# A linear-attention and mixture-of-experts kernel: scatters tied to the next group's tiles, |turns| on ScalarE, sines for two tiles at once, xT by tile, and another test of the decay

## The chip, the cores and the metric

The kernel runs on one core of a Trainium2 chip. The metric is the device time of the program in microseconds (us). The engines are named as the profile names them: PE (TensorE; PEld is its weight loading), ACT (ScalarE), DVE (VectorE), POOL (GpSimd) and SP (SyncE, which only issues transfers here). Each engine works through its own list of instructions in a fixed order and waits on semaphores for the others.

## The reference, cut to what matters

```python
# q, k, v, a_re, a_im: (batch 4, heads 8, seq 768, head_dim 48)
mag = sqrt(a_re**2 + a_im**2);  scale = minimum(mag, 0.999) / (mag + 1e-6)
ar, ai = a_re * scale, a_im * scale
for t in range(768):                      # per batch and head, a 48 x 48 complex state
    S_re, S_im = ar*S_re - ai*S_im + outer(k[t], v[t]),  ar*S_im + ai*S_re
    y[t] = q[t] @ S_re
x = y as (3072 tokens, 384)
logits = x @ w_gate + log1p(exp(x @ w_noise)) * noise      # 8 experts
top2, weights = two largest of a token, softmax over the two
out[token] += weight * (relu(x @ w1[e]) @ w2[e])           # w1: 384 x 1024, w2: 1024 x 384
```

## The kernel before, in words

The sequence is cut into 6 groups g of 128 steps; with 4 batches b that gives 24 tiles, n = 4g + b, each 128 rows by 384 columns (8 heads of 48). The recurrence is turned into matrix products: the decay's logarithm and its angle are summed along the 128 rows by a product with a triangular matrix, q and k are multiplied by e to the plus or minus of the summed logarithm and by the cosine and sine of the summed angle, and a tile's output is a masked 128 x 128 score matrix times v plus q times the state Z that came in from the group before.

The steps of a group, by the functions that the program lists at the end of this section:

- `p1` (for two tiles, 128 x 768): Ln of re, Exp of its negative (1/re), the tangent im/re, and the logarithm of the magnitude. A Relu of RE_MIN - re with a sum (tile `scr`) notes in `bad` whether some re lies under 0.6; with such a value, or a large tangent, a slow path at the end of the program would do the work again.
- `p2a`, `p2t`, `p2s`: Arctan; a product with `tri_t` that sums the angle in turns; rounding by adding a large constant (ACT, tile `tf`), the remainder (DVE, line 254), its absolute value by a bitwise and (DVE, line 255), then for each tile two sines of 384 columns, the cosine from the absolute value (tile `tr`).
- `p3`, `p3q`: a product with `tri_l`, Exp with both signs (`ee`), multiplied into `qk`, then `qh` and `kh`. One row of `ee` goes out to memory and comes back as the columns `ecol` of the group.
- `tr_unit`, `sc_unit`, `st_unit`: transposes of qh and kh into `qT` and `kT` (copied by ACT), scores `psc`, masked by DVE into `am`, and the state's product `pG`. `st_scale` multiplies two ecol columns into `fcol` and that into the state Z.
- `y_unit`: 16 products into `pY` (8 in the first group), copied by ACT into `xT` (line 347); `x_unit` transposes it back into token rows `xr`; `gate_logits` (tiles `lt`, `lz`) and `gate_dispatch` choose two experts for each token, compute a slot `sl` for each, and POOL scatters the rows to memory `xs` by 8 indirect transfers a group (line 408).

The eight experts follow: `load_x` fetches an expert's rows (`xga`, `xgb`), `x_T` transposes them, `mm1` and `mm2` are the two layers with weights split into a high and a low part, and the result is added to `out` by gathers and scatters of POOL.

Ln and Exp need another activation table than Arctan and Sin, so ACT's table functions run in phases: `phase` numbers them, and extra dependencies hold each table load behind the whole phase before. A table of steps (`at`, with the numbers of `P`) says at which tile's step a function is emitted, so that p1, p2 and p3 of a group run some tiles ahead of the tiles that use them. From this emission order, with a higher priority for `x_unit`, `gate_logits` and `gate_dispatch`, the framework makes each engine's list by its own estimate of when operands are ready; the lists that result are quoted below.

`xT` is one buffer of 128 x 4 x 4 x 128 for a whole group: the first `y_unit` of a group writes a buffer that `x_unit` and `gate_logits` of the group before still read.

Of the kernel before, what the change touches and what calls it, by code (L numbers as in the profile page):

```python
# [24 lines left out]
RE_MIN = 0.6  # L25
# [51 lines left out]
def kernel(  # L77
# [57 lines left out]
    b_re = cp.tile([128, 1], F32, name="b_re")  # L135
    nc.vector.memset(b_re, RE_MIN)
# [43 lines left out]
    for t in ecol:  # L180
        nc.vector.memset(t, 0.0)
# [8 lines left out]
    XT, W = {}, {}  # L190
# [29 lines left out]
    def p1(m):  # L220

        T0[m] = [pf.tile([128, 2, HD], F32, name=f"t0{i}", bufs=2) for i in range(3)]
        ta, tb, th = (flat(x) for x in T0[m])
        ph = 2 * (2 * m // B)
        re, im = flat(RE[m]), flat(IM[m])
        phase(ph, ta, re, AF.Ln)
        phase(ph, tb, ta, AF.Exp, scale=-1.0)
# [4 lines left out]
        nc.scalar.activation(sc, re, AF.Relu, scale=-1.0, bias=b_re, accum_out=bad[:, 0, i:i + 1])
# [1 line left out]
        nc.vector.scalar_tensor_tensor(ta, ta, 2.0, tb, op0=OP.mult, op1=OP.add)
# [13 lines left out]
    def p2t(n):  # L248
        b, g = bt(n)
        pt = psC.tile([128, 512], F32, name="cum")  # L250
        nc.tensor.matmul(pt[:, :HD], tri_t, T0[n // 2][2][:, b % 2, :], start=True, stop=True)  # L251
# [1 line left out]
        nc.scalar.activation(TF[n][:, 1, :], pt[:, :HD], AF.Identity, bias=b_rnd)
        nc.vector.scalar_tensor_tensor(TF[n][:, 0, :], TF[n][:, 1, :], -RND, pt[:, :HD], op0=OP.add, op1=OP.subtract)
        nc.vector.tensor_scalar(TF[n][:, 1, :].bitcast(I32), TF[n][:, 0, :].bitcast(I32), 0x7FFFFFFF, None,
                                op0=OP.bitwise_and)
# [21 lines left out]
    def p3q(n, i):  # L278
        tr = TR[n].rearrange("p r (h d) -> p r h d", h=H)
        nc.vector.tensor_mul((qh, kh)[i][n % NQ][:, :, :, 0:D].rearrange("p h r d -> p r h d"),  # L280
                             QK[n][:, i, :].rearrange("p (h d) -> p h d", h=H)[:, None].to_broadcast([128, 2, H, D]),
                             tr)
# [29 lines left out]
    def st_upd(n):  # L312
        b, g = bt(n)
        if g + 1 == NG:
            return
        if g:
            nc.vector.tensor_add(Z[b], Z[b], pG)
        else:
            Z[b] = pa.tile([112, H, D], F32, name=f"z{b}")
            nc.vector.tensor_copy(Z[b], pG)  # L320

    def st_scale(n):
        b, g = bt(n)
# [3 lines left out]
        nc.vector.tensor_mul(f, ecol[g % 3][:, b, :], ecol[(g + 1) % 3][:, b, :])
        nc.vector.tensor_mul(Z[b], Z[b], f[:, :, None].to_broadcast([112, H, D]))

    def y_unit(n):  # L330

# [15 lines left out]
        nc.scalar.activation(XT[g][:, :, b, :], pY, AF.Copy)  # L347
# [66 lines left out]


# [142 lines left out]
    for g in range(NG):  # L558
        f = B * g + .5
        q1, q2, q3 = P.get(f"s{g}", (P["p1"], P["p2"], P["p3"]))  # L560
        for j in range(B // 2):
# [4 lines left out]
            at(f - q2, p2carry, m)  # L566
        for j in range(B):
# [292 lines left out]
```

## Time and profile before

| | |
|---|---|
| median of 3 runs | 743.57 us (743.0 to 745.0) |
| the profiled execution | 743.21 us, span 741.5 us |
| mean granted TensorE clock | 0.992 |
| PE / PEld busy | 702.5 us (95%) / 623.5 us (84%) |
| DVE / ACT / POOL busy | 418.6 (56%) / 346.6 (47%) / 169.5 us (23%) |
| attention (to the last xT) | about the first 262 us |
| the eight experts | the rest |

How to read it: the shares are means over two stages with different limits. In the expert stage PE is busy without a gap and ACT and DVE for less than half of the time; in the attention stage ACT and DVE are about as busy as PE. A matmul's end is modelled, so that a stretch in which PE counts as busy can still have room in it; the number of matmuls in a stretch and the busy time of PEld say more.

### The profile page before, as it was taken

The page shows a single profiled execution, that of the slowest core. Times are in us where ns is not written, and L with a number is a line of the kernel's source. Part 1 is how long each engine was busy: PE and PEld are TensorE (multiplying, and loading weights), DVE is VectorE, ACT ScalarE, POOL GpSimd, SP SyncE. Part 2 cuts the span into 40 slices and gives each one's busy share as a digit, 9 for nine tenths or more (in the row PEclk, how much of TensorE's full clock was granted, in tenths as well). Part 3 has the DMA queues.
Part 4 walks back from the last instruction along what each step waited for, and adds up shares of the span by engine and source line. Part 5 has one row for each costly group of instructions (what it writes and reads, how often), then busy time and mean ns, then how long its engine had stood idle before and what let it go on. Part 6 is the DMA issues. An engine that isn't in the chain of part 4 may idle for free. (4 is left out here: it accounts for less than half of the span.)

```text
span 741.5 us, 13540 instructions
## 1 busy us (share of the span) xinstructions
PE 702.5 (95%) x5184; PEld 623.5 (84%) x5184; DVE 418.6 (56%) x960; ACT 346.6 (47%) x633; POOL 169.5 (23%) x187
## 2 busy tenths in 40 slices
PE   0799989999999899999999999999999999999995
PEld 0467778979788779989988998997998998998995
DVE  5698999989998373554353444425425525435311
ACT  7999999987966330443133223323304303413300
POOL 2000005130524341022123124024024023122212
PEclk9999999999999999999999999999999999999998
DMA  8476966643367432262244235226226135131101
GB/s 299 104 250 168 290 198 217 184 165 88 112 191 242 147 133 94 68 232 80 96 155 122 86 111 174 75 87 212 74 89 201 40 122 186 33 105 56 50 33 34
DMA packets 64090, 100.18 MB, mean 135 GB/s; under 512 B 26490, under 2 KB 46129, under 8 KB 64016
## 3 DMA queue, kind: packets, MB, share of 16 engines
q1 hardware_dynamic: 54464, 71.68, 31.0%
q0 software_dynamic: 9552, 27.54, 10.7%
q8 instruction: 43, 0.70, 0.4%
q14 instruction: 31, 0.25, 0.1%
HBM read 68.55 MB, written 32.08 MB: 136 GB/s over the span
## 5 line engine op out<-in xcount | busy, mean ns | idle before, releaser
L535 PE MATMUL po<-w2h,h 128*128 128x384 f32 x768 | 201.7, 339 | 0.0
L511 PE MATMUL ph<-x,w1h 128*128 128x320 f32 (+1 forms) x720 | 192.4, 351 | 0.3 <-ACT x L498 0.3
L535 PEld LDWEIGHTS po<-w2h,h 128*128 128x128 f32 x768 | 139.9, 188 | 0.1
L511 PEld LDWEIGHTS ph<-x,w1h 128*128 128x128 f32 x720 | 126.7, 188 | 15.6 <-ACT x L498 0.5
L516 DVE SCALAR_TENSOR_TENSOR h<-ph,h 128x256 fp32r<-128x256 f32 (+2 forms) x184 | 74.2, 432 | 99.9 <-ACT h L513 99.9
L535 PE MATMUL po<-w2l,h 128*128 128x384 f32 x384 | 129.6, 337 | 0.0
L549 POOL DMA_INDIRECT out_dram<-ao,ox x56 | 55.7, 995 | 319.4 <-DVE ao L548 277.6
L511 PE MATMUL ph<-x,w1l 128*128 128x320 f32 (+1 forms) x360 | 125.5, 349 | 0.0
L513 ACT ACTIVATE h<-ph 128x320 fp32r<-128x320 f32 (+1 forms) x120 | 61.5, 512 | 119.8 <-PE ph L511 114.4
L548 DVE SCALAR_TENSOR_TENSOR ao<-po,gw,ao 128x384 f32<-128x384 f32 (+1 forms) x56 | 34.5, 616 | 134.3 <-PE po L535 133.4
L408 POOL DMA_INDIRECT xs<-xr,sl x48 | 57.0, 1187 | 199.2 <-DVE kh L280 106.9
L498 ACT CAST x<-px 128x320 fp32r<-128x320 f32 (+1 forms) x45 | 21.9, 502 | 126.7 <-PE px L496 125.9
L511 PEld LDWEIGHTS ph<-x,w1l 128*128 128x128 f32 x360 | 67.6, 188 | 7.3
L535 PEld LDWEIGHTS po<-w2l,h 128*128 128x128 f32 x384 | 72.1, 188 | 0.1
L522 POOL DMA_INDIRECT ao<-out_dram,ox x49 | 49.0, 999 | 37.3 <-DMA out_dram<-ao,ox 24.5
L300 PE MATMUL psc<-qT,kT 112*128 112x128 f32 x384 | 54.1, 277 | 0.0
L300 PEld LDWEIGHTS psc<-qT,kT 112*128 112x128 f32 x384 | 48.3, 191 | 2.7 <-issue 1.1
L464 ACT CAST w2h<-raw 128x768 fp32r<-128x768 f32 x32 | 25.3, 834 | 51.4 <-PE po L540 49.3
L346 PE MATMUL pY<-am,v 128*48 128x128 f32 x384 | 44.1, 280 | 4.5 <-DVE am L301 4.5
L344 PE MATMUL pY<-qT,z 112*48 112x128 f32 x320 | 38.2, 281 | 0.2 <-ACT xT L347 0.2
L346 PEld LDWEIGHTS pY<-am,v 128*48 128x48 f32 x384 | 31.5, 125 | 7.9 <-DVE am L301 5.7
L251 PE MATMUL cum<-t,tri_t 128*128 128x384 f32 x48 | 20.9, 559 | 17.9 <-ACT t L198 17.0
(204 smaller groups left out, 1038.0 us busy)
## 6 DMA issues: line engine op xcount, KB each, us to landing
raw<-in_moe_w_dram SPq DMA_DIRECT2D x24, 512.0 KB, 3.9
raw<-in_moe_w_dram SPq DMA_DIRECT2D x32, 384.0 KB, 3.8
qk<-in_qk_dram SPq DMA_DIRECT2D x24, 384.0 KB, 4.0
xga<-xs SPq DMA_DIRECT2D x8, 800.0 KB, 4.2
re<-in_a_dram SPq DMA_DIRECT2D x12, 384.0 KB, 5.3
im<-in_a_dram SPq DMA_DIRECT2D x12, 384.0 KB
v<-in_v_dram SPq DMA_DIRECT2D x24, 192.0 KB, 3.2
out_dram<-zero SPq DMA_DIRECT2D x12, 384.0 KB, 5.7
```

Source lines behind the costliest of these rows:

```text
L300: nc.tensor.matmul(p[:, j, :], KT[n][:, h, :], QT[n][:, h, :], start=True, stop=True)
L344: nc.tensor.matmul(o, Z[b][:, h, :], QT[n][:, h, :], start=True, stop=False, skip_group_check=True)
L346: nc.tensor.matmul(o, V[n][:, h, :], AM[n][:, h, :], start=not g, stop=True, skip_group_check=True)
L408: d = nc.gpsimd.indirect_dma_start(out=xs, out_offset=bass.IndirectOffsetOnAxis(ap=sl[:, kk, b:b + 1], axis=0), in_=XR[g][:, lo + b, :], i ...
L464: nc.scalar.copy(hi, raw_t)
L511: nc.tensor.matmul(p[:, :n], W1[kk][i][:, f * 128:(f + 1) * 128], XW[w, kk][:, j, :], start=(m == 0), stop=(m == len(ms) - 1))
L513: nc.scalar.activation(h[:, 0:n], p[:, :n], AF.Relu)
L516: nc.vector.scalar_tensor_tensor(h[:, dst:dst + b - a], p[:, a:b], 0.0, h[:, a:b].bitcast(F32), op0=OP.max, op1=OP.subtract)
L522: nc.gpsimd.indirect_dma_start(out=ao[j][0:w, :], out_offset=None, in_=out, in_offset=bass.IndirectOffsetOnAxis(ap=OX[e][0:w, j:j + 1], ax ...
L535: nc.tensor.matmul(p[:, :DM], HT[w, f][i][:, o:o + 128], W2[f // 2][k2][:, f % 2, :], start=(m == 0), stop=(m == len(ms) - 1))
L548: nc.vector.scalar_tensor_tensor(a, p[0:n, :DM], g, a, op0=OP.mult, op1=OP.add)
L549: nc.gpsimd.indirect_dma_start(out=out, out_offset=bass.IndirectOffsetOnAxis(ap=OX[e][0:n, j:j + 1], axis=0), in_=a, in_offset=None, bound ...
```

## The change

It has six parts.

1. **Scatters.** For groups 0 to 3, the scatters of tile b = 1, 2, 3 of a group get a dependency on ACT's xT copy of tile b - 1 of the next group.
2. **The test of re.** The Relu pass and its sum go. The Exp that gives 1/re sums its output on the way (`accum_out`), and the sum is compared with 1.6 x 768 at the end. Beside it DVE takes the minimum of each group's `ecol` (`decm`, 6 reductions of 112 x 32), compared with 1e-15.
3. **|turns| on ScalarE.** The bitwise and on DVE (24 of 128 x 384) goes; an Abs on ACT (12 of 128 x 768) takes its place.
4. **Sines for two tiles.** `tf` and `tr` hold two tiles; 48 sines of 384 columns become 24 of 768. `p2s` is emitted after the four `p2t` of its group, not after each.
5. **xT by tile**, in 6 buffers of 128 x 4 x 128.
6. **fcol by group.** One product of 112 x 32 for a group, where there was one of 112 x 8 for a tile (5 for 20).

```diff
-        phase(ph, tb, ta, AF.Exp, scale=-1.0)
+        i = 2 * m
+        phase(ph, tb, ta, AF.Exp, scale=-1.0, accum_out=bad[:, 0, i:i + 1])
         nc.vector.tensor_mul(th, im, tb)
-        i = 2 * m
         nc.vector.tensor_tensor_reduce(tb, th, th, 1.0, 0.0, OP.mult, OP.max, bad[:, 1, i:i + 1])
-        sc = pf.tile([128, 2 * HD], BF16, name="scr")
-        nc.scalar.activation(sc, re, AF.Relu, scale=-1.0, bias=b_re, accum_out=bad[:, 0, i:i + 1])
...
-        TF[n] = pf.tile([128, 2, HD], F32, name="tf", bufs=4)
-        nc.scalar.activation(TF[n][:, 1, :], pt[:, :HD], AF.Identity, bias=b_rnd)
-        nc.vector.scalar_tensor_tensor(TF[n][:, 0, :], TF[n][:, 1, :], -RND, pt[:, :HD], op0=OP.add, op1=OP.subtract)
-        nc.vector.tensor_scalar(TF[n][:, 1, :].bitcast(I32), TF[n][:, 0, :].bitcast(I32), 0x7FFFFFFF, None,
-                                op0=OP.bitwise_and)
+        if n % 2 == 0:
+            TF[n // 2] = pf.tile([128, 2, 2, HD], F32, name="tf", bufs=2)
+        tf = TF[n // 2][:, :, n % 2, :]
+        nc.scalar.activation(tf[:, 1, :], pt[:, :HD], AF.Identity, bias=b_rnd)
+        nc.vector.scalar_tensor_tensor(tf[:, 0, :], tf[:, 1, :], -RND, pt[:, :HD], op0=OP.add, op1=OP.subtract)
...
-    def p2s(n):
-        TR[n] = pq.tile([128, 2, HD], F32, name="tr", bufs=8)
-        phase(2 * (n // B) + 1, TR[n][:, 0, :], TF[n][:, 1, :], AF.Sin, scale=-TWO_PI, bias=b_cos)
-        phase(2 * (n // B) + 1, TR[n][:, 1, :], TF[n][:, 0, :], AF.Sin, scale=-TWO_PI)
+    def p2s(m):
+        f, a = (flat(TF[m][:, i]) for i in range(2))
+        nc.scalar.activation(a, f, AF.Abs)
+        TR[m] = pq.tile([128, 2, 2, HD], F32, name="tr", bufs=4)
+        phase(2 * (2 * m // B) + 1, flat(TR[m][:, 0]), a, AF.Sin, scale=-TWO_PI, bias=b_cos)
+        phase(2 * (2 * m // B) + 1, flat(TR[m][:, 1]), f, AF.Sin, scale=-TWO_PI)
...
+        if b == B - 1:
+            nc.vector.tensor_reduce(decm[0:112, g:g + 1], ecol[g % 3].rearrange("p b h -> p (b h)"), axis=AX.X, op=OP.min)
...
-        f = pa.tile([112, H], F32, name="fcol", bufs=2)
-        nc.vector.tensor_mul(f, ecol[g % 3][:, b, :], ecol[(g + 1) % 3][:, b, :])
-        nc.vector.tensor_mul(Z[b], Z[b], f[:, :, None].to_broadcast([112, H, D]))
+        if b == 0:
+            FC[g] = pa.tile([112, B, H], F32, name="fcol", bufs=2)
+            nc.vector.tensor_mul(FC[g], ecol[g % 3], ecol[(g + 1) % 3])
+        nc.vector.tensor_mul(Z[b], Z[b], FC[g][:, b, :, None].to_broadcast([112, H, D]))
...
-            XT[g] = pa.tile([128, H // 2, B, 128], F32, name="xT")
+        XT[n] = pa.tile([128, H // 2, 128], F32, name="xT", bufs=6)
...
-        nc.scalar.activation(XT[g][:, :, b, :], pY, AF.Copy)
+        YC[n] = nc.scalar.activation(XT[n], pY, AF.Copy)
...
+                if g < NG - 2 and b:
+                    behind.append((d, B * (g + 1) + b - 1))
...
+            at(f - q2 + .01, p2s, m)
...
-            at(f - q2 + j * P["dt"] + P["ds"], p2s, n)
...
+    later = mybir.DependencyInfo(mybir.DependencyClass.Sync, mybir.DependencyReason.SCHED_ONLY)
+    for d, n in behind:
+        tc.add_manual_dep(d.ins, YC[n].ins.name, later, reason="pace")
```

The lists of the engines move. On ACT, the first group's angle phase, from the table load ahead of Arctan on (`t_159` and the like are p1's tiles); before:

```order
L197 ACT_TABLE_LOAD
L198 ACTIVATE t_159<-t_159 128x768
L198 ACTIVATE t_173<-t_173 128x768
L232 ACTIVATE scr,bad<-re,b_re 128x768 x2
L253 ACTIVATE tf<-cum,b_rnd 128x384 x2
L198 ACTIVATE tr<-tf 128x384
L198 ACTIVATE tr<-tf,b_cos 128x384
L198 ACTIVATE tr<-tf 128x384
L198 ACTIVATE tr<-tf,b_cos 128x384
L253 ACTIVATE tf<-cum,b_rnd 128x384 x2
L198 ACTIVATE tr<-tf 128x384
L198 ACTIVATE tr<-tf,b_cos 128x384 x2
```

and with the change (its lines are numbered a little higher; L262 is Abs):

```order
L198 ACT_TABLE_LOAD
L199 ACTIVATE t_159<-t_159 128x768
L199 ACTIVATE t_171<-t_171 128x768
L254 ACTIVATE tf<-cum,b_rnd 128x384 x3
L262 ACTIVATE tf<-tf 128x768
L199 ACTIVATE tr<-tf 128x768
L254 ACTIVATE tf<-cum,b_rnd 128x384
L199 ACTIVATE tr<-tf,b_cos 128x768
L262 ACTIVATE tf<-tf 128x768
L199 ACTIVATE tr<-tf 128x768
L199 ACTIVATE tr<-tf,b_cos 128x768
```

The two Relu passes are gone from it, the third rounding now stands ahead of the first sine, and each Abs stands behind the remainders of two tiles.

Also on ACT, the rows ahead of tile 4's xT, the first of group 1. Before, it stands behind group 2's Exps and the copy `lt` of group 0's logits:

```order
L355 COPY xr<-cum 128x384
L197 ACT_TABLE_LOAD
L198 ACTIVATE ee<-cum 128x384 x4
L198 ACTIVATE t_1153<-re 128x768
L198 ACTIVATE ee<-cum 128x384 x4
L198 ACTIVATE t_1154<-t_1153 128x768
L366 COPY lt<-cum 128x128
L347 ACTIVATE xT<-pY 128x4x128
```

and with the change right behind group 2's Arctan, ahead of its sines and Exps (the first row is tile 3's xT, the last tile 4's):

```order
L352 ACTIVATE xT<-pY 128x512
L294 ACTIVATE qT<-ptr 112x512
L199 ACTIVATE t_661<-t_661 128x768
L294 ACTIVATE kT<-ptr 112x512 x2
L199 ACTIVATE t_661<-t_660,b_eps 128x768
L198 ACT_TABLE_LOAD
L199 ACTIVATE t_571<-t_571 128x768
L199 ACTIVATE t_662<-t_662 128x768
L352 ACTIVATE xT<-pY 128x512
```

Tile 4's xT moved past a whole angle phase and a whole Exp phase of ACT.

On DVE, where the attention ends and the first expert's rows are read (`gw` and `ox` come from the fetched rows `xga`; the `am` around them belong to tiles 22 and 23); before:

```order
L404 TENSOR_REDUCE sl_3304<-ga1oh 128x2
L301 TENSOR_TENSOR am<-psc,mask 128x512 x2
L489 COPY gw<-xga 128x4
L490 CAST ox<-xga 128x4
L301 TENSOR_TENSOR am<-psc,mask 128x512
L370 COPY lz<-cum 128x48
```

and with the change:

```order
L409 TENSOR_REDUCE sl_3214<-ga1oh 128x2
L303 TENSOR_TENSOR am<-psc,mask 128x512 x3
L497 COPY gw<-xga 128x4
L498 CAST ox<-xga 128x4
L375 COPY lz<-cum 128x48
```

One of tile 23's two masked halves now stands ahead of the copy that waits for the fetched rows; the other stays behind it.

More of the change, by code (lines that the diff above doesn't have):

```diff
@@ L24 @@
 LN2_LO = 1.4286068203094173e-06
-RE_MIN = 0.6
+RE_SUM = 1.6
+DEC_MIN = 1e-15
 TAN_MAX = 1.5
@@ L134 @@
     nc.vector.memset(b_cos, math.pi / 2.0)
-    b_re = cp.tile([128, 1], F32, name="b_re")
-    nc.vector.memset(b_re, RE_MIN)
     b_rnd = cp.tile([128, 1], F32, name="b_rnd")
@@ L160 @@
     nc.vector.memset(bad, 0.0)
+    decm = cp.tile([128, NG], F32, name="decm")
+    nc.vector.memset(decm, 1.0)
     ap = ctx.enter_context(ExitStack())
@@ L180 @@
     for t in ecol:
-        nc.vector.memset(t, 0.0)
+        nc.vector.memset(t, 1.0)
     pG = psA.tile([112, H, D], F32, name="pG", bufs=1)
@@ L189 @@
     QT, KT, AM, Z, XR, QKD = {}, {}, {}, {}, {}, {}
-    XT, W = {}, {}
+    XT, FC = {}, {}
     phases = {}
@@ L251, in p2t @@
         nc.tensor.matmul(pt[:, :HD], tri_t, T0[n // 2][2][:, b % 2, :], start=True, stop=True)
-        TF[n] = pf.tile([128, 2, HD], F32, name="tf", bufs=4)
-        nc.scalar.activation(TF[n][:, 1, :], pt[:, :HD], AF.Identity, bias=b_rnd)
-        nc.vector.scalar_tensor_tensor(TF[n][:, 0, :], TF[n][:, 1, :], -RND, pt[:, :HD], op0=OP.add, op1=OP.subtract)
-        nc.vector.tensor_scalar(TF[n][:, 1, :].bitcast(I32), TF[n][:, 0, :].bitcast(I32), 0x7FFFFFFF, None,
-                                op0=OP.bitwise_and)
-        if g + 1 < NG:
-            nc.sync.dma_start(car[:, b, :], TF[n][127:128, 0, :])
-    def p2s(n):
-        TR[n] = pq.tile([128, 2, HD], F32, name="tr", bufs=8)
-        phase(2 * (n // B) + 1, TR[n][:, 0, :], TF[n][:, 1, :], AF.Sin, scale=-TWO_PI, bias=b_cos)
-        phase(2 * (n // B) + 1, TR[n][:, 1, :], TF[n][:, 0, :], AF.Sin, scale=-TWO_PI)
+        if n % 2 == 0:
[3 more added lines that the diff above has]
+        nc.vector.scalar_tensor_tensor(tf[:, 0, :], tf[:, 1, :], -RND, pt[:, :HD], op0=OP.add, op1=OP.subtract)
+        if g + 1 < NG:
+            nc.sync.dma_start(car[:, b, :], tf[127:128, 0, :])
+    def p2s(m):
[4 more added lines that the diff above has]
+        phase(2 * (2 * m // B) + 1, flat(TR[m][:, 1]), f, AF.Sin, scale=-TWO_PI)
     def p3(n):
@@ L278, in p3q @@
     def p3q(n, i):
-        tr = TR[n].rearrange("p r (h d) -> p r h d", h=H)
+        tr = TR[n // 2][:, :, n % 2, :].rearrange("p r (h d) -> p r h d", h=H)
         nc.vector.tensor_mul((qh, kh)[i][n % NQ][:, :, :, 0:D].rearrange("p h r d -> p r h d"),
@@ L353, in x_unit, with gate_logits @@
         for i in range(H // 2):
-            nc.tensor.transpose(p[:, i * 128:(i + 1) * 128], XT[g][:, i, b, :], ident)
+            nc.tensor.transpose(p[:, i * 128:(i + 1) * 128], XT[n][:, i, :], ident)
         nc.scalar.copy(XR[g][:, b, 0:DM].rearrange("p (h d) -> p h d", h=H),
                        p.rearrange("p (h x) -> p h x", h=H)[:, :, 0:D])
-    def gate_logits(xT, lo, hi):
+    def gate_logits(g, lo, hi):
         n = hi - lo
@@ L362, in gate_logits @@
             for b in range(n):
-                nc.tensor.matmul(p[32 * b:32 * b + 32, 0:128], wg[:, i, :], xT[:, i, lo + b, :],
+                nc.tensor.matmul(p[32 * b:32 * b + 32, 0:128], wg[:, i, :], XT[B * g + lo + b][:, i, :],
                                  start=(i == 0), stop=(i == H // 2 - 1), tile_position=(0, 32 * b), skip_group_check=True)
@@ L377, in gate_tr @@
         return p
-    scat = []
+    scat, behind, YC = [], [], {}
     def gate_dispatch(g, lo, hi, lz):
@@ L423, in glog @@
     def glog(g, lo, hi):
-        LZ[g, lo] = gate_logits(XT[g], lo, hi)
+        LZ[g, lo] = gate_logits(g, lo, hi)
     def gdis(g, lo, hi):
@@ L657 @@
     nc.gpsimd.iota(lim, pattern=[[N, E]], base=CAP, channel_multiplier=0, allow_small_or_imprecise_dtypes=True)
-    nc.vector.tensor_scalar(bad[:, 0], bad[:, 0], 0.0, None, op0=OP.is_gt)
+    nc.vector.tensor_scalar(bad[:, 0], bad[:, 0], RE_SUM * 2 * HD, 0.5, op0=OP.is_le, op1=OP.is_lt)
+    nc.vector.tensor_scalar(decm, decm, DEC_MIN, None, op0=OP.is_lt)
+    nc.vector.tensor_reduce(bad[0:112, 0, 1:2], decm[0:112], axis=AX.X, op=OP.max)
     nc.vector.tensor_scalar(bad[:, 1], bad[:, 1], TAN_MAX ** 2, None, op0=OP.is_gt)
```

## The prediction, made before the changed kernel was run

> **What bounds the kernel now.** I read the windows first, since the page's shares mix two stages: columns are the window, then busy time and number of instructions of PE, PEld, DVE, ACT and POOL, the granted clock and the transfers' share.
>
> ```profile
> 28.00:115.00 87.00, 79.46 (x841) 64.02 (x842) 78.90 (x148) 81.57 (x151) 1.80 (x2) 0.98 0.71 214
> 115.00:191.00 76.00, 75.94 (x919) 64.09 (x917) 70.53 (x173) 65.89 (x126) 23.82 (x23) 1.00 0.51 157
> 191.00:231.00 40.00, 39.60 (x505) 34.56 (x504) 36.28 (x93) 30.12 (x61) 17.12 (x15) 1.00 0.58 177
> 400.00:500.00 100.00, 100.00 (x575) 94.62 (x574) 40.21 (x80) 27.91 (x49) 19.76 (x20) 1.00 0.30 99
> ```
>
> In the experts (last row) PE has no gap and ACT and DVE work less than half of the time, so nothing that the change touches counts there; if the attention ends earlier, the experts move forward by as much. In the attention the limits differ. From 28 to 115 us ACT works 81.57 of 87 us and PE gets 841 matmuls in, 9.7 a microsecond: ACT bounds. From 115 to 231 us PE counts as busy for 115.5 of 116 us with 12.3 matmuls a microsecond, and ACT and DVE follow at 83% and 92%. Ahead of 28 us stands the first group's chain, on which PE waits for its first 17 us.
>
> ```profile
> PE cum L251 <- ACT t L198: 17.0, 1, 17.0
> PE pY L346 <- DVE am L301: 4.5, 4, 3.0
> ```
>
> These two rows of the waits of PE (waiter, releaser, total, times, longest) say that beside the start the only long wait is one of 3.0 us for a mask product, which belongs to the end of the attention (below).
>
> **The change, part by part.** Prices of one instruction (mean ns before the last bar) are in these rows of the groups by form:
>
> ```profile
> L198 ACT ACTIVATE t<-t 128x768 f32<-128x768 f32 x36 | 29.8, 850 | 0.2
> L198 ACT ACTIVATE tr<-tf,b_cos 128x384 f32<-128x384 f32 x24 | 13.8, 615 | 0.5 <-DVE tf L255 0.5
> L198 ACT ACTIVATE tr<-tf 128x384 f32<-128x384 f32 x24 | 12.7, 527 | 0.1
> L198 ACT ACTIVATE t<-t,b_eps 128x768 f32<-128x768 f32 x12 | 11.2, 936 | 2.8 <-DVE t L234 2.8
> L232 ACT ACTIVATE scr<-re,b_re 128x768 bf16<-128x768 f32 x12 | 11.2, 934 | 0.3 <-DMA re<-in_a_dram 0.3
> L232 ACT ACTIVATION_READ_ACCUMULATOR scr<-re,b_re 128x1 f32 x12 | 2.4, 196 | 0.0
> L254 DVE SCALAR_TENSOR_TENSOR tf<-tf,cum 128x384 f32<-128x384 f32 x24 | 12.8, 550 | 8.2 <-ACT tf L253 7.7
> L255 DVE TENSOR_SCALAR tf<-tf 128x384 int32<-128x384 int32 x24 | 8.0, 362 | 0.1
> L327 DVE TENSOR_TENSOR fcol<-ecol,ecol 112x8 f32<-112x8 f32 x20 | 3.0, 158 | 0.1
> L404 DVE TENSOR_REDUCE sl<-ga4oh 128x8 uint32<-128x64 f32 x4 | 0.9, 214 | 0.0
> ```
>
> A group of four tiles loses on ACT two Relus with their readings, 2 x (934 + 196) = 2.26 us, and eight sines, 4 x (615 + 527) = 4.57 us. It gains two readings of the sum (0.39), four sines of 768, priced like Exp with and without a bias, 2 x (936 + 850) = 3.57 us, and two Abs at 850, 1.70 us. That is 6.83 against 5.66 us. Four instructions fewer give back 0.4 us of this, since on ACT one starts about 0.1 us before the last ends (3.97 + 0.84 = 4.81 against 4.72 in the rows below). ACT is relieved by 0.8 us a group, little, because the Abs comes to the busier engine. DVE loses 4 x 362 and 4 x 158 ns and gains one fcol and one minimum at some 0.2 us each, by the reduction at 214: 1.7 us a group.
>
> *To tile 7, the ACT-bound stretch.* Counted in ACT's two lists up to the xT of tile 7, before has 10 Relus and 24 sines, the change 8 sums, 12 sines and 6 Abs, and all other kinds stand in equal numbers (the Relus had been put ahead). 10 x 1.13 + 12 x 1.142 = 25.0 us against 8 x 0.196 + 6 x 1.786 + 6 x 0.85 = 17.4 us: 7.6 us less, 5.8 us with 18 instructions fewer. How much of it reaches the end differs by place. The start of ACT's timeline (start, duration):
>
> ```profile
> 3.97 0.84 ACT L198 ACTIVATE t<-re 128x768 f32<-128x768 f32 x1 [1.86 <-DMA re<-in_a_dram]
> 4.72 0.92 ACT L232 ACTIVATE scr<-re,b_re 128x768 bf16<-128x768 f32 x1
> 5.63 0.83 ACT L198 ACTIVATE t<-t 128x768 f32<-128x768 f32 x1
> 6.59 0.84 ACT L198 ACTIVATE t<-re 128x768 f32<-128x768 f32 x1
> 8.26 1.56 ACT L198 ACTIVATE t<-t 128x768 f32<-128x768 f32 x2
> 17.53 0.92 ACT L232 ACTIVATE scr<-re,b_re 128x768 bf16<-128x768 f32 x1
> 19.63 1.05 ACT L253 ACTIVATE tf<-cum,b_rnd 128x384 f32<-128x384 f32 x2
> 26.84 1.28 ACT L197 ACT_TABLE_LOAD   x1
> 17.04 2.90 PE L251 MATMUL cum<-t,tri_t 128*128 128x384 f32 x4 [17.04 <-ACT t L198]
> ```
>
> The second Ln starts at 6.59 though ACT was free at 6.46, so it seems to have waited for its load: the first Relu was hidden by that. The second one holds its Exp from 7.34 to 8.26, 0.9 us that come through the rest of the chain. The two Relus at 17.53 stood where ACT waits for the first angle product (half of PE's four, 17.04 + 1.45 = 18.5); the rounding could start 1.1 us sooner, but the new list puts a third rounding ahead of the first sine, and that one waits until a `cum` buffer is read out by DVE (550 ns) and filled again (1.45 us). I take 0.4 us, bounds a loss of 0.5 and a gain of 2. Together **-1.3 us**, between -0.4 and -3.8.
>
> Of the 5.8 us, 2.4 belong to these first 27 us (four Relus less four readings, 8 sines for 4, two Abs, 6 instructions: 4.5 - 0.8 + 4.6 - 3.6 - 1.7 - 0.6). The other 3.4 us lie where ACT is busy for 94% of the time; I take **-3.0 us**, bounds 0 and -3.4.
>
> *xT by tile.* In the old list tile 4's xT waits for group 0's logits, since they share the buffer:
>
> ```profile
> 72.64 0.62 ACT L347 ACTIVATE xT<-pY 128x512 f32<-128x512 f32 x1
> 96.60 0.33 ACT L366 COPY lt<-cum 128x128 f32<-128x128 f32 x1
> 96.74 0.69 ACT L347 ACTIVATE xT<-pY 128x512 f32<-128x512 f32 x1
> 104.49 0.60 ACT L347 ACTIVATE xT<-pY 128x512 f32<-128x512 f32 x1 [0.90 <-PE pY L346]
> 114.47 0.59 ACT L347 ACTIVATE xT<-pY 128x512 f32<-128x512 f32 x1
> ```
>
> These are the xT of tiles 3, 4, 6 and 7, with the logits' copy: 24 us without a finished tile, then a crowd. The new list has tile 4 ahead of group 2's sines, so PE's work is spread. What it is worth at most is what ACT idles in this window, 87 - 81.57 = 5.4 us; I take **-1.0 us**, for a list that is less lumpy, not shorter.
>
> *Tiles 8 to 19.* Three groups' relief, 5 us on DVE and 2.3 on ACT, meets a PE that counts as busy throughout. I take **-1.5 us**, bounds 0 and -5.
>
> *What the change adds.* An Abs waits for the remainders of two tiles; mostly one other ACT instruction stands between the second rounding and it, as long as one remainder (550 ns). If DVE comes at once nothing is lost; if the remainder stands behind a product of 0.95 us, 1.5 us are. For all 12 together I take **+1.0 us**, near the lower end, since the lists put the remainders right behind the roundings; behind a late Abs stand that phase's sines, its table load and its Exps, and for these wait qh, kh and PE.
>
> *The scatters' wait.* Behind a waiting scatter stand POOL's next scatters and the clearing of the row buffer two groups on. But in time they come late already:
>
> ```profile
> 112.89 1.17 POOL L408 DMA_INDIRECT xs<-xr,sl  x1 [106.92 <-DVE kh L280]
> 220.40 0.60 ACT L347 ACTIVATE xT<-pY 128x512 f32<-128x512 f32 x1 [0.71 <-PE pY L346]
> 228.18 1.60 POOL L408 DMA_INDIRECT xs<-xr,sl  x1 [0.30 <-ACT kT L292]
> 230.37 0.59 ACT L347 ACTIVATE xT<-pY 128x512 f32<-128x512 f32 x1
> ```
>
> Group 0's first scatter starts at 112.89, after the xT of tile 6 (104.49) for which its last must wait; group 3's last tile goes out at 228.18, after tile 18's xT at 220.40 (the last row is tile 19's). Each scatter is bound by its slots, not by the new wait: **0**, and its number on POOL and the transfers stay.
>
> *The end of the attention.*
>
> ```profile
> 248.91 0.97 POOL L408 DMA_INDIRECT xs<-xr,sl  x1 [0.31 <-issue]
> 257.06 0.17 DVE L489 COPY gw<-xga 128x4 f32<-128x4 f32 x1 [7.75 <-DMA xga<-xs]
> 257.94 0.57 PE L346 MATMUL pY<-am,v 128*48 128x128 f32 x4 [2.99 <-DVE am L301]
> ```
>
> DVE stands still until the first expert's rows have come, and tile 23's mask products stand behind that, so PE waits 2.99 us. In the new list one of the two is ahead of it, the other still behind, and the y unit needs both: **0**, bounds -3.0 and +1.
>
> The sum is -1.3 - 3.0 - 1.0 - 1.5 + 1.0 = -5.8 us. The profiled execution took 743.21 us for a span of 741.5, so 737.4; the median of the runs, 743.57, is 0.36 higher. I say **737.5 us**.
>
> **The rivals.** *Room in PE (larger gain).* If the shared xT buffer and a late DVE hold PE back from 115 us on, more comes free than 1.5 us. PEld works 98.65 of these 116 us, 85%, against 94.6% in the experts; filled as densely, the stretch would be 116 x (1 - 85.0/94.6) = 11.8 us shorter. Half of that in place of the 1.5 us gives 733. For it: the matmuls per microsecond vary between windows at equal busy time; against: the expert products are of another size. The Trainium skill says the same of this measure (Perfetto Trace Analysis, Identifying the Most-Contended Engine): matmul busy time is a poor sign of how near PE is to its limit, the weight load's share a better one; the trace agrees in that busy reads 99% at both densities.
>
> *Only the start (no change).* If the middle follows a loop through all three engines, in which a lighter ACT only waits longer, then -1.3 and a little stay: 742. For it: DVE at 91% in ACT's own window.
>
> *The Abs in ACT's way (slower).* Its place is the angle phase of each group, its price the wait for DVE. From 0.5 us more for each of the 12 the sum is used up; at 1.0 us more it is -5.8 + 12 = +6.2, 749.5. For it: before, only the cosine waited for line 255, and DVE is at 92%. Against: remainders were met in time so far (that row shows 0.5 us of wait in all 24).
>
> *The waits do nothing, or the list hurts elsewhere* is inside these: it alters no term.
>
> **How the numbers follow.** Forecast 0.45 (735 to 740.5), room in PE 0.2, only the start 0.2, the Abs 0.15. A measurement of this kernel tells about 0.3%, 2.2 us, from no change. The forecast and the larger gain lie below 741.3, faster 0.65; the third within, 0.2; slower 0.15. The range leaves out the far half of the larger gain and the last case: 731.5 to 744.5.
>
> **What would show it.** ACT's table load now at 26.84 should come at 25 to 26 us; tile 7's xT near 109; tile 19's (now 230.37) near 224 to 226; PE's long wait at the end of about 3 us again. Abs should have waits of DVE under 3 us in total, scatters none of ACT, the experts should take the same time from the last xT to the end. It is wrong if ACT idles more from 28 to 115 us, or if tile 7 is early and tile 19 is not.

## The result, and the profile after

The changed kernel takes 738.7 us (median of four runs, 738.59 to 739.76); the kernel before, beside it, 743.8 (743.0 to 745.0). The ratio is 0.9933, 95% interval 0.992 to 0.9946: 5.1 us faster, where 737.5 us was forecast. The number is nearly met. The places are not, so that the hit is in good part luck; most of this section and the next are about that.

The profiled execution of the changed kernel took 739.76 us for a span of 738.0. It is the longest of the four runs, so the two traces differ by 3.5 us of span and not by 5.1; loads that came late at the start, seen below, are part of that. The easiest way to find where they lie is ACT's copy of each tile, `xT<-pY`: its start tells when the tile left the attention. First before (tiles 0, 22 and 23; tiles 4, 6, 7 and 19 stand in the prediction), start and duration:

```profile
45.95 0.58 ACT L347 ACTIVATE xT<-pY 128x512 f32<-128x512 f32 x1
...
250.96 0.60 ACT L347 ACTIVATE xT<-pY 128x512 f32<-128x512 f32 x1 [1.31 <-PE pY L346]
261.12 0.60 ACT L347 ACTIVATE xT<-pY 128x512 f32<-128x512 f32 x1 [1.43 <-PE pY L346]
```

Then after, tiles 0, 4, 6, 7, 19, 22 and 23:

```profile
46.88 0.58 ACT L352 ACTIVATE xT<-pY 128x512 f32<-128x512 f32 x1
...
81.18 0.58 ACT L352 ACTIVATE xT<-pY 128x512 f32<-128x512 f32 x1
...
104.07 0.64 ACT L352 ACTIVATE xT<-pY 128x512 f32<-128x512 f32 x1
113.83 0.59 ACT L352 ACTIVATE xT<-pY 128x512 f32<-128x512 f32 x1
...
229.24 0.58 ACT L352 ACTIVATE xT<-pY 128x512 f32<-128x512 f32 x1
...
250.56 0.60 ACT L352 ACTIVATE xT<-pY 128x512 f32<-128x512 f32 x1 [1.31 <-PE pY L351]
257.31 0.60 ACT L352 ACTIVATE xT<-pY 128x512 f32<-128x512 f32 x1 [0.56 <-PE pY L351]
```

Differences of these starts, and of the span's end (741.5 and 738.0), give a table by stretch:

| stretch | before, us | after, us | difference | forecast |
|---|---|---|---|---|
| start to tile 0 | 45.95 | 46.88 | +0.93 | -1.3 |
| tile 0 to tile 7 | 68.52 | 66.95 | -1.57 | -4.0 |
| tile 7 to tile 19 | 115.90 | 115.41 | -0.49 | -1.5 |
| tile 19 to tile 22 | 20.59 | 21.32 | +0.73 | 0 |
| tile 22 to tile 23 | 10.16 | 6.75 | -3.41 | 0 |
| tile 23 to the end | 480.38 | 480.69 | +0.31 | 0 |

(The forecast's +1.0 for the Abs had no place of its own.) Tile 4 comes 15.6 us sooner and tile 7 only 0.6 us; and the step between tiles 22 and 23, where the forecast has nothing, has 3.4 of the 3.5 us, the others together 0.1.

The windows after, with the columns that the prediction names, and behind them the last window of the kernel before, which it did not show:

```profile
28.00:115.00 87.00, 80.11 (x845) 65.21 (x846) 75.43 (x137) 79.26 (x140) 0.48 (x1) 0.96 0.72 217
115.00:191.00 76.00, 75.21 (x924) 64.22 (x923) 67.45 (x158) 66.09 (x121) 23.49 (x24) 1.00 0.50 154
191.00:231.00 40.00, 39.84 (x502) 34.48 (x500) 35.20 (x90) 31.54 (x60) 14.36 (x14) 1.00 0.52 166
231.00:262.00 31.00, 29.09 (x321) 24.54 (x320) 20.12 (x98) 14.35 (x33) 9.87 (x11) 1.00 0.57 192
```

```profile
231.00:262.00 31.00, 27.51 (x292) 23.66 (x293) 16.51 (x84) 12.68 (x30) 8.80 (x11) 0.94 0.48 164
```

From 28 to 115 us ACT works 79.26 us instead of 81.57 and so idles 7.7 us instead of 5.4, while PE gets 845 matmuls in instead of 841: ACT's relief has become ACT's waiting. The waits say for whom (waiter, releaser, total, times, longest); before and after, over the whole span:

```profile
ACT kT L292 <- PE ptr L291: 5.5, 12, 0.7
DVE am L301 <- PE psc L300: 7.8, 5, 3.2
```

```profile
ACT kT L294 <- PE ptr L293: 9.2, 17, 1.3
DVE am L303 <- PE psc L302: 16.1, 12, 2.8
```

ACT waits longer for PE's transposes and DVE longer for PE's scores. At the end of the attention, DVE and PE after (the lines before are the last fence ahead of the prediction's sum):

```profile
251.64 0.69 DVE L303 TENSOR_TENSOR am<-psc,mask 128x512 f32<-128x512 f32 x1 [2.73 <-PE psc L302]
...
254.71 0.17 DVE L497 COPY gw<-xga 128x4 f32<-128x4 f32 x1 [2.38 <-DMA xga<-xs]
255.66 0.68 DVE L303 TENSOR_TENSOR am<-psc,mask 128x512 f32<-128x512 f32 x1
...
254.38 0.39 PE L351 MATMUL pY<-am,v 128*48 128x128 f32 x4
254.82 0.39 PE L351 MATMUL pY<-am,v 128*48 128x128 f32 x4
...
256.39 0.43 PE L351 MATMUL pY<-am,v 128*48 128x128 f32 x4 [0.96 <-DVE am L303]
```

and PE before, behind its wait of 2.99 us:

```profile
258.72 0.65 PE L346 MATMUL pY<-am,v 128*48 128x128 f32 x4
```

One mask product of tile 23 now stands ahead of the weights copy `gw<-xga`; the rows for that copy are also there 2.35 us sooner (254.71 against 257.06). PE does half of its work on tile 23 with the first product (254.38, 254.82) and then waits 0.96 us, not 2.99. And four matmuls take 0.39 us there, not 0.65: before, the wait was followed by a lower granted clock (0.94 for the whole window, 1.00 now). Two microseconds of wait and some 1.4 of slow matmuls are the 3.4 us.

How much of this is the list's order and how much the earlier rows can be read from the second mask product, for which half of the products with `am` wait. Here it is before (after, it is the row at 255.66 above), and behind it the slots of group 4 with the next logits `lz`, before and after:

```profile
258.60 0.68 DVE L301 TENSOR_TENSOR am<-psc,mask 128x512 f32<-128x512 f32 x1
```

```profile
238.82 0.17 DVE L370 COPY lz<-cum 128x16 f32<-128x16 f32 x1 [1.25 <-PE cum L368]
...
238.97 0.20 DVE L404 TENSOR_REDUCE sl<-ga3oh 128x6 uint32<-128x48 f32 x1
```

```profile
236.93 0.19 DVE L409 TENSOR_REDUCE sl<-ga3oh 128x6 uint32<-128x48 f32 x1
...
237.91 0.17 DVE L375 COPY lz<-cum 128x16 f32<-128x16 f32 x1
```

The second product starts 2.94 us sooner. It stands 1.54 us behind the copy before and 0.95 after, since the first product no longer lies between; so 0.59 of the 2.94 us are this place in the list, and 2.35 are the rows. From its start to tile 23's xT it takes 1.65 us instead of 2.52, and this is the clock. Half of the 2.35 us can be followed back to the slots, which come 2.04 us sooner: in the old list they stand behind `lz`, on which DVE waits 1.25 us for PE, in the new list ahead of it. When the load of the rows is issued 1.17 us of this are left (250.45 against 251.62). The other half is the load itself, which takes 4.3 us to DVE's copy instead of 5.4; no run shows the reason.

### The profile page after: what moved, and what is told of

Same layout as the page of the kernel before. It is cut to its first block, busy times and chain, and to the rows that moved or that the text cites. A ratio compares the mean times of both kernels' runs of the same rounds, so it can differ in the third digit from the quotient of the medians.

```text
span 738.0 us, 13470 instructions
## 1 busy us (share of the span) xinstructions
PE 699.7 (95%) x5184; PEld 622.5 (84%) x5184; DVE 411.3 (56%) x929; ACT 342.5 (46%) x609; POOL 166.1 (23%) x187
## 5 line engine op out<-in xcount | busy, mean ns | idle before, releaser
L519 PEld LDWEIGHTS ph<-x,w1h 128*128 128x128 f32 x720 | 126.7, 188 | 15.6 <-ACT x L506 0.5
L413 POOL DMA_INDIRECT xs<-xr,sl x48 | 53.7, 1118 | 200.6 <-DMA xd<-xr 108.6
L351 PE MATMUL pY<-am,v 128*48 128x128 f32 x384 | 42.6, 275 | 4.1 <-DVE am L303 4.1
L303 DVE TENSOR_TENSOR am<-psc,mask 128x512 f32<-128x512 f32 x48 | 32.6, 687 | 16.2 <-PE psc L302 16.1
```

What stands on the lines that cost most here:

```text
L303: nc.vector.tensor_mul(AM[n][:, 4 * half:4 * half + 4, :], p, mask[:, None, :].to_broadcast([128, 4, 128]))
L351: nc.tensor.matmul(o, V[n][:, h, :], AM[n][:, h, :], start=not g, stop=True, skip_group_check=True)
L413: d = nc.gpsimd.indirect_dma_start(out=xs, out_offset=bass.IndirectOffsetOnAxis(ap=sl[:, kk, b:b + 1], axis=0), in_=XR[g][:, lo + b, :], i ...
L519: nc.tensor.matmul(p[:, :n], W1[kk][i][:, f * 128:(f + 1) * 128], XW[w, kk][:, j, :], start=(m == 0), stop=(m == len(ms) - 1))
```

## The experiments

**How they can be read.** The experiments ran on other chips than the two kernels above. There the kernel before itself took 756 to 774 us, with medians between 762 and 770, because stalls come in from some 122 us on that the first chip does not have (their rows stand below, under what was not expected). So whole times are given with their intervals, but a difference of a few microseconds in them is not evidence on the change. The first 115 us are free of these stalls: from the xT of tile 0 to that of tile 7 the kernel before took 68.52 us on the first chip and 68.54 and 68.53 in two runs on another that alter only the end; the changed lists took 66.95, 66.95 and 66.97. This **stretch from tile 0 to tile 7** is the measure, good to a few hundredths. A second, coarser one is ACT's **angle phase** of the first group, between its second and third table load: 12.08 us before, 12.48 after. Equal lists differ in it by up to 0.7 us (12.08, 12.09 and 11.41 in before, e1 and e2; 11.16 and 11.90 in e9 and e12).

| run | what | tile 0 to 7, us | angle phase, us | time, us | ratio to before, 95% |
|---|---|---|---|---|---|
| | before | 68.52 | 12.08 | | |
| | changed | 66.95 | 12.48 | | |
| e1 | before, copy behind one product | 68.54 | 12.09 | 767.9 | 0.998 (0.994 to 1.002) |
| e2 | before, copy behind both | 68.53 | 11.41 | 767.2 | 1.000 (0.996 to 1.004) |
| e3 | changed, copy behind both | 66.95 | 12.49 | 770.8 | 1.005 (1.001 to 1.008) |
| e4 | changed, scatters don't wait | 66.97 | 12.49 | 771.7 | 1.006 (1.003 to 1.009) |
| e5 | before + sines | 71.78 | 13.50 | 764.9 | 1.000 (0.996 to 1.004) |
| e6 | e3 + eight useless Relus | 71.03 | 12.48 | 764.2 | 0.995 (0.991 to 0.999) |
| e7 | before without Relus | 66.95 | 11.16 | 766.3 | 0.998 (0.994 to 1.001) |
| e8 | before + xT by tile | 69.86 | 12.09 | 760.0 | 0.987 (0.981 to 0.993) |
| e9 | e7 + xT by tile | 68.63 | 11.16 | 780.4 | 1.015 (1.011 to 1.019) |
| e10 | e5 + xT by tile | 71.78 | 13.50 | 775.3 | 1.009 (1.005 to 1.014) |
| e11 | changed, group 0's gate later | 65.68 | 12.48 | 751.9 | 0.986 (0.979 to 0.994) |
| e12 | e9, group 0's gate later | 66.99 | 11.90 | 770.8 | 1.013 (1.004 to 1.022) |

Runs e1 to e4 shared a chip, e5 and e6 had one each, e7 to e12 shared another, e11 and e12 at a later time. Theory B is the prediction's: ACT bounds the first 115 us, and its relief is the gain. Theory A: the gain is made at the end of the attention.

**e1, e2, e3: the end of the attention.** The weights copy `gw` is made to follow tile 23's mask products in DVE's list, by a dependency without a wait (e1: half 0; e2 and, in the changed kernel, e3: half 1).

```
+        AMI[n, half] = nc.vector.tensor_mul(AM[n][:, 4 * half:4 * half + 4, :], p, ...)
...
+        gwc = nc.vector.tensor_copy(GW[e][:, js[0]:js[-1] + 1], src_t[:, :, DM + e])
...
+    tc.add_manual_dep(GWC[0].ins, AMI[NT - 1, 1].ins.name, after, reason="order")
```

> The kernel before with one edit: the first expert's weights copy (gw<-xga) stands behind the first of tile 23's two mask products on DVE, as in the changed kernel; nothing else of the change. Theory A (the gain is made at the end of the attention): PE's wait there falls from 2.99 us to about 1 us, the four-matmul rows after it from 0.65 to about 0.4 us, and the time falls by 2 to 3 us, to 741 to 742. Theory B (the gain comes from ACT's relief in the first 115 us, as predicted): the second product still stands behind the copy, PE waits on, and the time stays within 1 us of 743.8.

> The kernel before with the copy gw<-xga behind both of tile 23's mask products. Theory A: PE's long wait is gone, the end of the attention is 3 to 4 us earlier, 740 to 741. Theory B: the wait of 2.99 us is removed, but the first expert's rows arrive no earlier and hold the experts' start up in its place: within 1 us of 743.8.

> The changed kernel with the copy gw<-xga behind both of tile 23's mask products. Theory A: the 0.96 us that PE still waits there goes, 737.5 to 738 against 738.7. If the experts wait for their rows instead: 738.7 as the changed kernel.

The times of e1 and e2 are not told apart from the kernel before; e3, at 1.005, stands beside e4 at 1.006, which has the changed kernel's lists and not this edit. But these runs could not have shown more, for two reasons. The edit moves `gw` alone, and the copy `ox` reads the same rows: in the lists that came out, `ox` stands ahead of both of tile 23's products in e1 and e2, and ahead of the second in e3, so that DVE still waits for the rows in front of them. In e2:

```profile
276.46 0.17 DVE L494 CAST ox<-xga 128x4 uint32<-128x4 f32 x1 [2.59 <-DMA xga<-xs]
276.60 0.69 DVE L303 TENSOR_TENSOR am<-psc,mask 128x512 f32<-128x512 f32 x1
```

And the wait of PE that they were to remove is not there on these chips: tiles 8 to 22 come later by the stalls, and the expert's rows come early enough. In e7, whose list has the copy ahead of both products as in the kernel before, the matmuls of tile 23 run at full speed, and tile 22 to tile 23 takes 5.58 us, as in e1 and e2:

```profile
272.07 0.17 DVE L487 COPY gw<-xga 128x4 f32<-128x4 f32 x1 [3.40 <-DMA xga<-xs]
274.14 0.39 PE L344 MATMUL pY<-am,v 128*48 128x128 f32 x4
```

So these runs do not tell the theories apart by their times. What they add is a floor: that step takes 5.6 us where nothing waits, against 10.16 before and 6.75 after. By the traces of the first chip the end was worth 3.4 us; no run has confirmed it, none has separated the order of the list from the earlier rows, and up to 1.2 us may still lie there.

**e4: the scatters without their wait.** The lists of all engines stay the same.

```
-        tc.add_manual_dep(d.ins, YC[n].ins.name, later, reason="pace")
+        pass
```

> The changed kernel without the scatters' wait for a tile of the next group; every engine's list stays the same. The prediction costs this wait at 0: 738.4 to 739.1, as the changed kernel. A rival has the wait hold up POOL's scatters (the trace of the changed kernel puts 20.9 us of POOL's idle time down to ACT's xT): then the groups' scatters start up to some us earlier without it, and if that counts for the end, the time falls to 737 or below; or, scatters that start earlier collide with loads and it rises over 739.7.

POOL's waits after, and in e4:

```profile
POOL xs L413 <- ACT xT L352: 20.9, 2, 20.6
```

```profile
POOL xs L413 <- ACT xT L352: 31.6, 1, 31.6
```

The row that looks like the scatters' new wait is in e4 too, where no such wait exists: it names what ended last before the scatter, not what the scatter waited for. In each kernel a group's first scatter starts 1.0 to 1.2 us behind its slots `sl` (after: 219.96 and 220.96 for group 3). The changed kernel's own trace shows more: within each of groups 0 to 3, every scatter behind the first starts 0.30 or 0.31 us after the one before it ends, and the xT copy that a tied scatter waits for ended 9 us or more earlier (closest in group 3: tile 18's at 220.89, the scatter at 229.87). e4 against e3 is within their intervals. The wait costs nothing, as forecast.

**e5: the sines alone.** The part of the change in `p2t`, `p2s` and `p3q`: the Abs on ACT, sines of two tiles; Relus, shared xT and scatters as before.

> The kernel before with one part of the change: the Abs on ACT and the sines of two tiles at once (the Relus, the shared xT and the scatters as before). Its list on DVE has one mask product of tile 23 ahead of the first expert's weights copy, as the changed kernel. Theory A (the gain is made at the end of the attention): most of the gain of 5.1 us comes with this part, 740 to 741.5 against 743.8. Theory B (the gain is ACT's relief, of which the Relus are the larger share): 1 us or less of gain, 742.8 to 744.

Neither theory has this: the angle phase grows by 1.42 us and the stretch to tile 7 by 3.26. ACT's list in that phase, e5:

```profile
20.00 1.05 ACT L255 ACTIVATE tf<-cum,b_rnd 128x384 f32<-128x384 f32 x2
21.67 0.84 ACT L263 ACTIVATE tf<-tf 128x768 f32<-128x768 f32 x1 [0.62 <-DVE tf L256]
22.90 0.58 ACT L255 ACTIVATE tf<-cum,b_rnd 128x384 f32<-128x384 f32 x1 [0.39 <-PE cum L251]
24.18 0.58 ACT L255 ACTIVATE tf<-cum,b_rnd 128x384 f32<-128x384 f32 x1 [0.70 <-PE cum L251]
24.66 0.92 ACT L198 ACTIVATE tr<-tf,b_cos 128x768 f32<-128x768 f32 x1
```

Before, the first sine starts at 20.83, 1.2 us behind the first rounding; here the first of a pair at 24.66, because two remainders, an Abs and two more roundings come first. While ACT waits for these (0.62, 0.39 and 0.70 us) it has no single sines to fill in.

**e7, e8, e9, e10: one part, and two.** e7 has no Relus, and sums 1/re instead:

```
-        phase(ph, tb, ta, AF.Exp, scale=-1.0)
+        phase(ph, tb, ta, AF.Exp, scale=-1.0, accum_out=bad[:, 0, i:i + 1])
-        sc = pf.tile([128, 2 * HD], BF16, name="scr")
-        nc.scalar.activation(sc, re, AF.Relu, scale=-1.0, bias=b_re, accum_out=bad[:, 0, i:i + 1])
```

e8 has the change's lines for `XT[n]` alone, e9 these and e7's, e10 these and e5's.

> The kernel before with one part of the change: re is checked by the sum of 1/re, and there are no Relus (the minimum of ecol is left out, so a very small decay is not looked for). Measure: the start of tile 7's xT, since what follows is lengthened by stalls on the chips of these runs. It stood at 114.47 before (114.57 and 113.84 in the first two runs) and at 113.83 after (112.90, 113.42). Theory B (ACT's work bounds this stretch, at the price of the eight useless Relus, 4.5 us for four of 0.85): ten Relus of 1.13 less eight readings of 0.2 are 9.7 us of ACT, some of it hidden at the start: 106 to 110. Theory C (the order of the lists bounds it, ACT's work only through it): 112 to 115.

> The kernel before with one part of the change: an xT of its own for each tile. It stands 31 instructions earlier on ACT for tile 4, and the number of instructions stays. Theory B: the work on ACT is the same, tile 7's xT stays at 113.5 to 114.5 (the prediction's -1.0 at most 113). Theory C (spreading PE's work): 109 to 112.5.

> The kernel before with both: the sum of 1/re in place of the Relus (without the minimum of ecol) and xT by tile; the sines as before. The sines alone put tile 7's xT 5.4 us later. If the parts add up, this one stands 5.4 us ahead of the changed kernel, at 107.5 to 109, and would be some 5 us faster than it where no stalls follow. If the sines' loss is one of the list without xT by tile, 111.5 to 114.

> The kernel before with the paired sines and the Abs and with xT by tile; the Relus stay. If the parts add up, the sines' 5.4 us less what xT by tile brings: 115 to 119. If xT by tile takes away the sines' loss: 112 to 114.5, and the Relus' removal then brings little in the changed kernel (112.9 to 113.8).

Without the Relus the stretch is 1.57 us shorter, with xT by tile 1.34 longer, with the sines 3.26 longer: added up +3.0 us. The whole change, which has all three, gives -1.57. The parts do not add up at all: the sines cost 3.26 us in the old list, 1.92 on top of xT by tile (e10 against e8), and gain 1.68 us on top of both others (the changed kernel against e9). This last step also brings fcol by group and the minimum of `ecol`, which no run tests alone, so the 1.68 us are not shown to be the sines' own. e8 (117.17) and e10 (119.54) have tile 7 later than any of their expectations; e9, from which 107.5 to 109 was expected if the parts add up, has it at 113.48. What holds it there is in PE's timeline of e9 and of e8, and in the windows of e9 behind it:

```profile
107.20 0.17 PE L392 MATMUL cum<-ohs,tri_b 128*128 128x8 bf16 x1 [2.09 <-DVE ohs L385]
```

```profile
110.09 0.17 PE L394 MATMUL cum<-ohs,tri_b 128*128 128x8 bf16 x1 [2.34 <-DVE ohs L387]
```

```profile
105.00:110.00 5.00, 2.91 (x28) 2.44 (x27) 4.87 (x15) 3.31 (x5) 0.00 (x0) 0.71 0.83 268
110.00:115.00 5.00, 5.00 (x38) 4.28 (x37) 2.00 (x5) 2.69 (x5) 0.30 (x1) 0.61 0.53 171
```

With xT by tile, PE comes to the end of tile 6 early, and there it waits for DVE, which first chooses group 0's experts (`ohs`) and then makes tile 7's mask products. In e9 the granted clock falls to 0.61 behind this wait. The changed kernel has the same wait, of 1.27 us:

```profile
109.48 0.17 PE L399 MATMUL cum<-ohs,tri_b 128*128 128x8 bf16 x1 [1.27 <-DVE ohs L392]
```

**e11, e12: group 0's gate later.** The changed kernel and e9, with the gate's due time moved so that tile 7's mask products stand ahead of it on DVE.

```
-            at(B * g + hi + .5 + P["gd"], gdis, g, lo, hi)
+            at(B * g + hi + .5 + P["gd"] + (1.5 if g == 0 else 0), gdis, g, lo, hi)
```

> The changed kernel with one edit: group 0's gate (the choice of experts and the slots, on DVE) is due one and a half tiles later, so that both of tile 7's mask products stand ahead of it on DVE. Theory G (what reaches tile 6 early is given back where PE waits for the gate and the products behind it, 1.27 us in the changed kernel): the wait goes, tile 7's xT at 110 to 112 against 112.9 to 113.8. Rival: DVE itself is full there, the work only changes places: 112.5 to 114. The time by the stalls of these chips: no verdict is expected.

> The kernel before with the sum of 1/re in place of the Relus, xT by tile, and group 0's gate due one and a half tiles later; the sines as before, the minimum of ecol left out. Without the later gate PE waited 2.09 us and then ran at a granted clock of 0.61 to 0.71; tile 6's xT stood at 99.86 and tile 7's at 113.48. Theory G: tile 7's xT at 108 to 110.5, the clock stays at 1.00. Rival: 112.5 to 114 as before.

PE has no wait over 0.5 us between 104 and 115 us in either, the clock stays at 1.00, and the stretch is 1.27 us shorter in e11 and 1.64 in e12. That is just the wait of the changed kernel, and less than the 2.09 us and the slow clock of e9: there tile 6 comes 57.75 us behind tile 0 instead of 55.01, so most of the work only changes places, as the rival had it. Part of tile 4's 15.6 us was thus given back at the gate, 1.3 us by the trace of e11. e11 had the lowest time of all kernels on these chips, 751.9; whether it beats the changed kernel is open, as the two never ran on one chip.

**e6: a price for ACT's time.** e3 with useless Relus.

```
         nc.vector.tensor_mul(th, im, tb)
+        if m >= 4:
+            sc = pf.tile([128, 2 * HD], BF16, name="scr")
+            nc.scalar.activation(sc, re, AF.Relu, scale=-1.0)
```

> The changed kernel with the copy gw<-xga behind both of tile 23's mask products (as in the third run) and eight useless Relus of 768 columns on ACT (0.85 us each, 6.8 us in all, none of them in the first group; four stand ahead of the xT of tile 5, all ahead of that of tile 11). Theory B (ACT bounds the stretch to tile 7, the prediction's -3.0): the four early ones alone cost 3 us, the time rises by 3 to 6 us against the third run's kernel, and tile 7's xT comes some 3 us later. Theory A (the order and the loop through three engines bound it): the rise is 1 us or less, and tile 7's xT moves by less than 1 us.

Six of the eight fell ahead of tile 7's xT, the last two of them at 107.20 and 108.86 us. To tile 5 four of them, 3.4 us of ACT, cost 1.0 us (counted from tile 0), to tile 7 all six, 5.1 us, cost 4.1. So work added to ACT is paid for by a third early on and by four fifths to tile 7; the six Relus that e7 lacks between tile 0 and tile 7, 6.0 us with their readings and less those of four sums (6 x 1.13 - 4 x 0.2), brought 1.57 us. Neither is a price of ACT's time alone, since the lists of ACT and DVE change their order with the Relus: from tile 6 to tile 7, e6 takes 2.6 us more than e3 for two Relus of 1.7. The two runs fit an ACT that is close to the bound with DVE and PE close behind, where what is added is paid and what is taken away is soon caught by the next engine; they do not show it.

## Why the prediction was right, and where it was not

The time and its sign were right; the sum that gave them was so by errors that cancel.

*The start, -1.3 (-0.4 to -3.8).* The step is wrong in sign for its angle phase. For the Relu that held the second Exp 0.9 us were taken, and 0.68 came: from the second Ln to the second table load it took 14.76 - 6.59 = 8.17 us before and 14.78 - 7.29 = 7.49 after (7.49 in e4 and e6 too, 7.80 in e3). But the angle phase was to gain 0.4 us and lost 0.40: in other traces it is 0.92 shorter without the Relus (e7, e9; 0.18 in e12) and 1.42 longer with the sines (e5, e10). So -0.28 up to the third table load, outside the range given for this term. Of the rest of the table's +0.93, 0.70 is a late load (the second Ln at 7.29 after a wait of 1.12 us, against 6.59), which the removed Relu no longer covers; in e3, with the same list there, it came at 6.12. The last 0.51 us lie between the third table load and tile 0, where the same lists differ by 0.8 us (19.62 after, 19.54 in e3, 18.84 in e4; 19.11 before); the granted clock was lower there after, 0.57 and 0.58 from 28 to 32 and from 32 to 36 us, against 0.67 and 0.90 before. e3 has tile 0 at 45.95, just as before: that any of this term reaches tile 0 is not shown.

*To tile 7, -3.0, and xT by tile, -1.0.* Together -1.57. The failing step is "the other 3.4 us lie where ACT is busy for 94% of the time", so that they arrive. The prediction's own test, that it is wrong if ACT idles more from 28 to 115 us, came true: 7.7 us against 5.4. Three of its other signs failed too: the third table load at 27.26 (25 to 26 expected), tile 7's xT at 113.83 (near 109), tile 19's at 229.24 (224 to 226). With ACT busy for 94%, DVE for 91% and PE for 91% of the window, 1.6 us arrived. And the Abs and the sines, priced by work alone, have an order: a pair's sines wait for both tiles. xT by tile did not shorten this stretch by itself, it lengthened it by 1.3 us, through the gate on DVE.

*Tiles 8 to 19, -1.5 (0 to -5).* -0.49: within its bounds, near the end for "only the start". This rival named the mechanism, a loop through three engines in which a lighter ACT waits longer; without the step from tile 22 to 23 the trace has -0.1 us, and 742 would have been near.

*The Abs, +1.0.* The row of the Abs shows no wait on DVE after, and the sines of 768 columns beside it, 941 and 848 ns, are priced as taken:

```profile
L262 ACT ACTIVATE tf<-tf 128x768 f32<-128x768 f32 x12 | 10.2, 846 | 0.0
```

Its cost came as lateness of the first tile of a pair, not as a wait in front of the Abs. The slower rival looked at the right place, and in the old list it would have come true for the first 115 us (e5: +3.3 us). With the other two parts it does not.

*The scatters' wait, 0.* Right, as the scatters' rows after and e4 show.

*The end of the attention, 0 (-3.0 to +1).* This is the term that was mis-sized, and it carries the result: -3.41. The step "one of the two is ahead of it, the other still behind, and the y unit needs both" is right as far as it goes: the second product does set the end, and its place in the list brought only 0.59 us. What the step took at nothing is that the rows themselves come sooner, 2.35 us, about half of it because the new list has group 4's slots ahead of the next logits. And the slow matmuls behind a wait of 3 us, 0.65 against 0.39 us, belonged into the price of that wait, some 1.4 us; with them even the lower bound was too small. On the clock, the Trainium skill (TensorE: Matmul & The Clock Gate, The HAM clock gate) has TensorE fall to half clock after an idle window of about 3.4 us, on windows that run free of the kernel. The trace agrees that a wait can be followed by slow matmuls at about half clock (0.52 from 258 to 260 us before, 0.50 from 108 to 112 in e9), but waits of 2.99 and 2.09 us were enough here, while 2.34 us in e8 left the clock at 1.00.

*Room in PE, 733.* Did not come: the matmuls per microsecond from 115 to 231 us rose from 12.28 to 12.29.

## What to carry to other kernels

An edit has no price of its own where three engines are busy for over 90%: the same three parts summed to +3.0 us one by one and came to -1.6 us in the whole change, so price the list that comes out, and read it at the next engine that would have to be faster too. A wait on TensorE costs its length and, in some of the traces here, slow matmuls behind it. Where a wait is for a load, ask not only what stands behind the wait, but also whether the new list lets the load start sooner. A forecast that meets the time should still be read stretch by stretch, since this one met it with its largest gain at a place that it had priced at nothing.

## What the runs showed that was not expected

On four other chips the kernel before took 756 to 774 us instead of 743 to 745, and the trace shows where: while POOL issues the scatters of a group, ACT and DVE stop and PE nearly does. The window from 122 to 124 us, before on the first chip and e1, whose lists are the same there:

```profile
122.00:124.00 2.00, 2.00 (x30) 1.65 (x28) 2.00 (x4) 2.00 (x5) 1.70 (x2) 1.00 0.58 160
```

```profile
122.00:124.00 2.00, 1.05 (x7) 0.53 (x7) 0.00 (x0) 0.00 (x0) 1.70 (x2) 1.00 0.54 206
```

and the instructions with which DVE and ACT go on in e1, here and at group 2's scatters, with one of PE's at group 3's:

```profile
125.25 0.96 DVE L282 TENSOR_TENSOR kh<-qk,tr 128x768 f32<-128x768 f32 x1 [3.51 <-remote]
125.36 0.48 ACT L357 COPY xr<-cum 128x384 f32<-128x384 f32 x1 [3.94 <-remote]
...
201.60 0.55 DVE L319 TENSOR_TENSOR z<-z,pG 112x384 f32<-112x384 f32 x1 [7.68 <-remote]
201.68 1.05 ACT L255 ACTIVATE tf<-cum,b_rnd 128x384 f32<-128x384 f32 x2 [7.91 <-remote]
...
239.96 0.47 PE L356 MATMUL cum<-ident,xT 128*128 128x128 f32 x1 [5.68 <-issue]
```

"remote" and "issue" stand where the profile sees nothing that would release the engine. In e1 the scatters of groups 0 to 3 run from 113 to 124, 149 to 161, 190 to 200 and 230 to 242 us. The stretches of over 1 us in which DVE and ACT stand still together begin, between 100 and 240 us, at 121.7, 154.3, 193.9 and 234.7, all inside these. The trace of the first chip has none there. What stops the engines is not settled: no run left the scatters out. It has a consequence for the result: the stalls fall at other places in other lists, and the times of these lists differ by more than the change brings (on one chip 780.4 us in e9 and 751.9 in e11). On one such chip the changed kernel's lists (e4) came out 0.3 to 0.9% slower than the kernel before. The gain of 0.7% is shown for a chip without the stalls, and for no other.

The other surprise is how exactly the first 115 us repeat: the second Ln, which waits for a load, starts at 7.29, 6.12 and 7.63 us in three traces of these lists, on two chips, and it is still 66.95, 66.95 and 66.97 us from tile 0 to tile 7.
